# A kernel of attention and two expert layers: the experts' sums of tokens made at the end of the projection before, the first expert's results scaled afterwards

## The chip, the cores and the metric

The kernel runs on one core of one Trainium2 chip. The metric is the device time of one execution in microseconds (us), the median of several runs.

## The reference

Attention over 16 heads (2 batches of 8) with 576 positions of 64, then a gated layer, then eight experts that all see every token, mixed by a matrix P that is normalised by rows and columns eight times. All in float32.

```python
q_rot, k_rot = rotate(q), rotate(k)
scores = np.matmul(q_rot, k_rot.transpose(0, 1, 3, 2)) / np.sqrt(64)
attn = softmax(scores)                      # rows of 576
x = np.matmul(attn, v)                      # as 1152 tokens of 512

g = x @ w_gate                              # 512 -> 1536
x = (g / (1 + np.exp(-g)) * (x @ w_val)) @ w_out   # wo: 1536 -> 512

logits = x @ w_gate2                        # 512 -> 8
P = np.exp(logits - logits.max())
for _ in range(8):
    P /= P.sum(1, keepdims=True) + 1e-9
    P /= P.sum(0, keepdims=True) + 1e-9
    P *= N / E
for e in range(8):                          # 512 -> 1024 -> 512
    out += P[:, e:e+1] * (np.maximum(x @ w1[e], 0) @ w2[e])
```

## The kernel before

Four stages follow each other: the attention (eight pairs of heads, to about 165 us), gate and value (`gv`, to about 320 us), the projection with w_out, here called wo (to 395 us), and the experts.

Every large matmul is made of three, since operands are split into a high and a low part (`xh` and `xl`, `wh` and `wl`): high by high, high by low, low by high (`mm3`). ScalarE makes the high part by a cast, VectorE the low part by a subtraction (`sub`). Weights of gate, value and wo come as 64-bit numbers. `convert` turns a unit of 1024 of them into two parts: one load, two ScalarE and seven VectorE instructions.

wo goes over four blocks `d` of 128 outputs and three blocks `c` of 384 tokens, each 36 matmuls into one PSUM bank `po`. ScalarE casts a bank into `xh`, VectorE makes `xl` from it.

The experts are 16 passes `n`, two per expert, each over 512 of the 1024 hidden units. The first matmul of a pass is made in a form with seven products in place of eight for a 2 by 2 block (halves of the 512 inputs by halves of tokens): `product` numbers them 1 to 7, each 6 matmuls of 288 columns. Products 3, 5, 6 and 7 need sums and differences of quarters of x: `sums(c)` makes them for token block `c` (0 or 1, 576 tokens each) from `x32`, which is `xh + xl` again in one piece, and splits them into `sh` and `sl`. `plain` makes products 1 and 2, `rest` the other five, with VectorE's additions (`add`) between them. A relu leaves `hh` and `hl`. Then `w2_tile` makes one tile of y (128 tokens by 512, 12 matmuls) at a time; nine make a pass. VectorE multiplies it with the column of `Pm` of its expert and adds it to `acc`.

The gate, which makes `Pm`, runs inside the first pass as a generator: its TensorE instructions are put between others, one step at each count in `GSTEPS`. A step of the eight rounds is a `pc` matmul on TensorE, then eight small VectorE operations that end in the next `Pm`. While `Pm` is not ready, the y tiles of pass 0 stay in PSUM (list `y`).

The order on TensorE is that of the code. On the other engines a scheduler of the framework sets it when the kernel is built; each engine does its instructions strictly in that order. Pools of SBUF stand on each other like a stack; a pool that is opened where others lay waits until these are done with. The pools of the experts (`hp`, `sp`, `ep`, `wp2` and others) lie where `up` with the gated values `uh` and `ul` was.

Of the kernel before, what the change touches and what calls it, by code (L numbers as in the profile page):

```python
# [29 lines left out]
GSTEPS = {17, 20} | {24 + 4 * i for i in range(10)}  # L30
# [27 lines left out]
def fused(ctx, tc, qk, v, rope, wgv, wo, wg2, w1, w2, out):  # L58
# [55 lines left out]
    def convert(src, hi, lo, wide=False):  # L114
# [14 lines left out]
        last = nc.vector if wide else nc.gpsimd  # L129
# [390 lines left out]
    def gated(x, x2, ps, W, W1):  # L520
        nonlocal cvp
        with ExitStack() as st:
            cvp = pool("cvp", bufs=2, stack=st)
            up = pool("up", stack=st)
            tp = pool("tp", bufs=2, stack=st)
            uh = [up.tile([128, NT], F32R, name=f"uh{f}") for f in range(KF)]
            ul = [up.tile([128, NT], F32R, name=f"ul{f}") for f in range(KF)]

            def gv(f, c):
                if f not in W:  # L530
                    W[f] = load_w64(wgv[f])
                w = W[f]
                ts = slice(c * CH, c * CH + CH)
                pg = ps.tile([128, 512], F32, tag="a", name="pg")[:, 0:CH]
                pv = ps.tile([128, 512], F32, tag="a", name="pv")[:, 0:CH]
                for o, dst in ((0, pg), (512, pv)):
                    for kk in range(KD):
                        mm3(dst, w, (slice(None), slice(o + kk * 128, o + kk * 128 + 128)),
                            x, (slice(None), kk, ts), kk == 0, kk == KD - 1)
                sg = tp.tile([128, CH], F32, tag="sg", name="sg")  # L540
                nc.scalar.activation(out=sg, in_=pg, func=AF.Silu)
                nc.vector.tensor_tensor(out=sg, in0=pv, in1=sg, op=ALU.mult)
                nc.scalar.copy(out=uh[f][:, ts], in_=sg)
                sub(ul[f][:, ts], sg, uh[f][:, ts])

            order = [(f, c) for f in range(KF) for c in range(NC)]
            for f in range(2):
                if f not in W:
                    W[f] = load_w64(wgv[f])
            for n, (f, c) in enumerate(order):  # L550
                if c == 0 and f + 2 < KF and f + 2 not in W:
                    W[f + 2] = load_w64(wgv[f + 2])
                gv(f, c)
            O = {}
            nc.sync.dma_start(out=wr, in_=wg2)
            nc.scalar.copy(out=wg[:, :, 0], in_=wr)
            sub(wg[:, :, 1], wr, wg[:, :, 0])

            def o_unit(i):
                if i * 8 < KD * KF and i not in O:  # L560
                    O[i] = load_w64(wo[:, i * WU:(i + 1) * WU])

            o_unit(0)
            o_unit(1)
            xh, xl = x2
            for d in range(KD):
                for c in range(NC):
                    if d == KD - 1 and c == 0:
                        W1[0, 0] = winograd_w(load_raw(w1[0, :, 0:WU]))
                    ts = slice(c * CH, c * CH + CH)  # L570
                    po = ps.tile([128, 512], F32, tag="a", name="po")[:, 0:CH]
                    for kk in range(KF):
                        i, o = divmod(d * KF + kk, 8)
                        o_unit(i + 1)
                        mm3(po, O[i], (slice(None), slice(o * 128, o * 128 + 128)),
                            (uh[kk], ul[kk]), (slice(None), ts), kk == 0, kk == KF - 1)
                    nc.scalar.copy(out=xh[:, d, ts], in_=po)
                    sub(xl[:, d, ts], po, xh[:, d, ts])


    def experts(x, ps, W1):
# [3 lines left out]
        nonlocal cvp  # L585
        cvp = pool("raw", bufs=3)
        hp = pool("hp")
        sp = pool("sp")
        ep = pool("ep")
        wp2 = pool("wp2", bufs=2)  # L590
        p1p = pool("p1p", bufs=5)
        dp = pool("dp", bufs=3)
# [3 lines left out]
        x32 = ep.tile([128, KD, NT], F32, tag="acc", name="x32")  # L596
        Pm = ep.tile([128, NTT, E], F32, name="Pm")
# [14 lines left out]
        def halves(c):  # L612

            o = 2 * HC * c
            return slice(o, o + HC), slice(o + HC, o + 2 * HC), slice(HC * c, HC * c + HC)

        def sums(c):

            a, b, o = halves(c)
            r = slice(a.start, b.stop)  # L620
# [8 lines left out]
            def low(i):  # L629
                sub(sl[:, i, :, o], s[i], sh[:, i, :, o])  # L630
# [17 lines left out]
        def product(n, u, c, i, po):  # L648
# [6 lines left out]
            if n == 0:  # L655
                gate_step()
# [241 lines left out]
```

## Time and profile before

| | before |
|---|---|
| median of 3 runs | 1181.37 us (1178.01 to 1184.85) |
| the profiled execution | 1178.95 us |
| its span | 1177.2 us |
| TensorE (PE) busy | 1145.4 us, 97% |
| VectorE (DVE) busy | 818.2 us, 70% |
| ScalarE (ACT) busy | 378.7 us, 32% |
| GpSimd (POOL) busy | 90.0 us, all in the first 230 us |

The span is the profiled execution from its first to its last instruction; the time also has what lies around it. Busy shares are means over stages with different limits, so they are to be read by stage. PEclk is the share of TensorE's full clock that was granted. An engine's row can name what it waited for ("<-DVE Pm").

### The profile page before, as it was taken

To read this page: it belongs to the slowest core of one execution; us is meant where nothing else is said; L and a number is where in the kernel's file an instruction comes from. 1 tells how busy PE (TensorE), PEld (TensorE's weight loads), DVE (VectorE), ACT (ScalarE), POOL (GpSimd) and SP (SyncE) were. 2 spreads that over 40 slices of the span, in tenths; PEclk is the share of its full clock that TensorE was granted. 3 is DMA by queue.
4 is the path that set the end of the run, shared out by engine and by line. 5 is a ranking of instruction groups with operands and counts; after the bars stand their busy time and mean duration, and the time that the engine had idled before them with its cause. 6 is when DMAs were issued, how large, how long until landed. Compare 5 with 4: busy or idle time off the path is not lost.

```text
span 1177.2 us, 16921 instructions
## 1 busy us (share of the span) xinstructions
PE 1145.4 (97%) x6840; PEld 1033.7 (88%) x6840; DVE 818.2 (70%) x1380; ACT 378.7 (32%) x623; POOL 90.0 (8%) x88
## 2 busy tenths in 40 slices
PE   7999999999999888999999999999999999999998
PEld 6767779999999786988989989989899899898997
DVE  7787759998842696857757658567586585685763
ACT  4667654443311440312313223123122232131220
POOL 5567300000000000000000000000000000000000
PEclk7999999999999988999999999999999999999999
DMA  5876413333211100111111111111111111111002
GB/s 161 235 209 164 113 72 108 107 108 108 72 55 52 56 18 19 55 54 36 51 46 49 36 36 55 54 36 55 54 36 37 37 53 55 36 55 54 18 1 80
DMA packets 24125, 80.62 MB, mean 68 GB/s; under 512 B 4272, under 2 KB 4784, under 8 KB 21872
## 3 DMA queue, kind: packets, MB, share of 16 engines
q1 hardware_dynamic: 24048, 79.56, 22.4%
q8 instruction: 53, 0.87, 0.3%
q14 instruction: 24, 0.20, 0.0%
HBM read 64.80 MB, written 2.36 MB: 57 GB/s over the span
## 4 chain that ended last, share of the span: by engine, by line
PE 90%; DVE 5%; DMA 2%; issue 1%; SPq 1%; ACT 1%; POOL 0%; DVEq 0%
PE p L719 11%; PE p L720 11%; PE p L721 11%; PE s L268 4%; PE pv L380 3%; PE t L308 2%; PE po L159 2%; PE po L161 2%; PE po L160 2%; PE pg L161 2%; PE pg L159 2%; PE pv L161 2%; PE pg L160 2%; PE pv L159 2%; PE pv L160 2%
## 5 line engine op out<-in xcount | busy, mean ns | idle before, releaser
L719 PE MATMUL p<-wh,hh 128*128 128x512 f32 x576 | 226.4, 393 | 0.0
L720 PE MATMUL p<-wl,hh 128*128 128x512 f32 x576 | 225.6, 392 | 0.0
L721 PE MATMUL p<-wh,hl 128*128 128x512 f32 x576 | 225.5, 391 | 0.0
L100 ACT CAST wh<-raw 128x768 fp32r<-128x768 f32 (+1 forms) x96 | 94.0, 982 | 366.7 <-PE p L721 259.9
L728 DVE SCALAR_TENSOR_TENSOR acc<-p,Pm,acc 128x512 f32<-128x512 f32 x135 | 101.1, 749 | 156.6 <-PE p L721 156.6
L67 DVE TENSOR_TENSOR wl<-raw,wh 128x768 fp32r<-128x768 f32 (+1 forms) x96 | 108.6, 1131 | 41.6 <-ACT wh L100 40.6
L721 PEld LDWEIGHTS p<-wh,hl 128*128 128x128 f32 x576 | 109.0, 189 | 22.9
L719 PEld LDWEIGHTS p<-wh,hh 128*128 128x128 f32 x576 | 109.1, 189 | 22.2
L720 PEld LDWEIGHTS p<-wl,hh 128*128 128x128 f32 x576 | 109.1, 189 | 22.1
L663 ACT ACTIVATE hh<-d 128x1152 fp32r<-128x1152 f32 (+1 forms) x68 | 74.6, 1098 | 126.1 <-DVE d L668 126.0
L664 DVE SCALAR_TENSOR_TENSOR hl<-d,hh 128x1152 fp32r<-128x1152 f32 (+1 forms) x68 | 85.8, 1263 | 21.9 <-ACT hh L663 21.9
L273 DVE TENSOR_REDUCE ng<-s 128x1 f32<-128x576 f32 x72 | 54.0, 753 | 19.2 <-PE s L268 17.2
L289 ACT ACTIVATE p<-s,ng 128x576 f32<-128x576 f32 x64 | 47.6, 743 | 26.8 <-DVE ng L273 26.7
L111 DVE TENSOR_TENSOR raw<-raw 128x256 f32<-128x256 f32 x128 | 53.3, 417 | 0.7
L159 PE MATMUL pg<-xh,wh 128*128 128x384 f32 x144 | 48.8, 339 | 3.3 <-ACT wh L140 2.6
L160 PE MATMUL pg<-xl,wh 128*128 128x384 f32 x144 | 48.7, 338 | 0.0
L161 PE MATMUL pg<-xh,wl 128*128 128x384 f32 x144 | 48.6, 338 | 0.0
L160 PE MATMUL pv<-xl,wh 128*128 128x384 f32 x144 | 48.3, 335 | 0.0
L159 PE MATMUL pv<-xh,wh 128*128 128x384 f32 x144 | 48.3, 335 | 0.0
L161 PE MATMUL pv<-xh,wl 128*128 128x384 f32 x144 | 48.1, 334 | 0.0
L159 PE MATMUL po<-uh,wh 128*128 128x384 f32 x144 | 48.1, 334 | 0.0
L160 PE MATMUL po<-ul,wh 128*128 128x384 f32 x144 | 48.1, 334 | 0.0
(3328 smaller groups left out, 2692.8 us busy)
## 6 DMA issues: line engine op xcount, KB each, us to landing
raw<-in_w SPq DMA_DIRECT2D x64, 512.0 KB, 3.9
raw<-in_wgv SPq DMA_DIRECT2D x11, 1024.0 KB, 4.9
x<-in_qk SPq DMA_DIRECT2D x15, 576.0 KB, 4.7
raw<-in_wo SPq DMA_DIRECT2D x6, 1024.0 KB, 4.8
x<-hl SPq DMA_DIRECT2D x42, 144.0 KB, 3.7
x<-hl SPq DMA_DIRECT2D x14, 288.0 KB, 4.1
v<-in_v SPq DMA_DIRECT2D x8, 320.0 KB, 4.9
out<-acc SPq DMA_DIRECT2D x9, 256.0 KB, 2.0
```

The costliest lines, as they stand in the source:

```text
L67: (eng or nc.vector).tensor_tensor(out=out_, in0=a, in1=hi.bitcast(F32), op=ALU.subtract)
L100: nc.scalar.copy(out=hi[:, 0:n], in_=raw[:, 0:n])
L159: nc.tensor.matmul(ps, wh[wsl], xh[xsl], start=first, stop=False)
L160: nc.tensor.matmul(ps, wh[wsl], xl[xsl], start=False, stop=False)
L161: nc.tensor.matmul(ps, wl[wsl], xh[xsl], start=False, stop=last)
L273: nc.vector.tensor_reduce(out=R[n, u], in_=SC[n, u][:, :, 0:288], axis=AX.XY, op=ALU.max, negate=True)
L663: nc.scalar.activation(out=hh[:, f, ts], in_=src, func=AF.Relu)
L664: nc.vector.scalar_tensor_tensor(out=hl[:, f, ts], in0=src, scalar=0.0, in1=hh[:, f, ts].bitcast(F32), op0=ALU.max, op1=ALU.subtract)
L719: nc.tensor.matmul(po, hh[:, f, tl], wh[:, ws], start=f == 0, stop=False)
L720: nc.tensor.matmul(po, hh[:, f, tl], wl[:, ws], start=False, stop=False)
L721: nc.tensor.matmul(po, hl[:, f, tl], wh[:, ws], start=False, stop=f == 3)
L728: nc.vector.scalar_tensor_tensor(out=acc[:, t], in0=po, scalar=Pm[:, t, e:e + 1], in1=acc[:, t], op0=ALU.mult, op1=ALU.add)
```

## The change

- wo's tail: ScalarE also copies each bank `po` as float32 into `x32`. `sums` no longer adds `xh` and `xl`.
- `token_sums` makes the four sums in place in `x32`, one after the other; the casts and low parts follow.
- The first pass is done in another order: all products of the first 576 tokens and y tiles 0 to 3, then the second 576 and tiles 4 to 8. Each group stays together, and the logits stand between the `plain` parts of block 0 and 1.
- The y tiles of pass 0 are copied to `acc` by ScalarE as they are. Pass 1, the second half of the same expert, is added; afterwards the whole `acc` is scaled by `Pm` in place.
- `GSTEPS`: the steps of the gate are spread over passes 0 and 1.
- `up` and the experts' pools lie on the right side of SBUF, in an order in which what is needed first lies over the `uh`, `ul` that are free first, and wait tile by tile (`reuse_waits="tile"`).
- wo's weights are loaded and converted in units of 512, in the buffers of the experts' raw weights (`raw`, three of 4 KB), where a unit of 1024 had its own.

```diff
-GSTEPS = {17, 20} | {24 + 4 * i for i in range(10)}
+GSTEPS = {10, 14, 18} | {24 + 6 * i for i in range(9)}
...
-    def load_w64(src):
+    def load_w64(src, n=WU):
         hi, lo = new_w()
-        for _ in convert(src, hi, lo, wide=True):
-            pass
+        for cs in (slice(i, i + n) for i in range(0, WU, n)):
+            for _ in convert(src[:, cs], hi[:, cs], lo[:, cs], wide=n == WU):
+                pass
...
+            cvp = pool("raw", bufs=3, reuse_waits="tile")
+            ep = pool("ep", reuse_waits="tile")
+            x32 = ep.tile([128, KD, NT], F32, tag="acc", name="x32")
+            w_out(x2, x32, ps, uh, ul, W1)
...
+    def token_sums(x32, c):
+        a, b, _ = token_halves(c)
+        a11, a12, a21, a22 = (x32[:, k:k + 2, ts] for ts in (a, b) for k in (2, 0))
+        for o, p, q, op in ((a22, a21, a22, ALU.add), (a21, a11, a21, ALU.subtract),
+                            (a11, a22, a11, ALU.subtract), (a12, a12, a11, ALU.subtract)):
+            nc.vector.tensor_tensor(out=o, in0=p, in1=q, op=op)
+        return a22, a11, a21, a12
...
-                O[i] = load_w64(wo[:, i * WU:(i + 1) * WU])
+                O[i] = load_w64(wo[:, i * WU:(i + 1) * WU], 512)
...
                 nc.scalar.copy(out=xh[:, d, ts], in_=po)
                 sub(xl[:, d, ts], po, xh[:, d, ts])
+                nc.scalar.copy(out=x32[:, d, ts], in_=po)
...
+        sp, hp, wp2, p1p, dp, sm = (pool(name, bufs=bufs, side="right", reuse_waits="tile") for name, bufs in
+                                    (("sp", 1), ("hp", 1), ("wp2", 2), ("p1p", 5), ("dp", 3), ("small", 1)))
...
         def sums(c):
-            nc.vector.tensor_tensor(out=x32[:, :, r], in0=xh[:, :, r].bitcast(F32), in1=xl[:, :, r].bitcast(F32), op=ALU.add)
+            s = token_sums(x32, c)
+            o = token_halves(c)[2]
+            for i in (1, 2, 0, 3):
+                nc.scalar.copy(out=sh[:, i, :, o], in_=s[i])
                 sub(sl[:, i, :, o], s[i], sh[:, i, :, o])
...
             if n == 0:
-                y.append((po, t))
+                nc.scalar.copy(out=acc[:, t], in_=po)
+            elif n == 1:
+                add(acc[:, t], po, acc[:, t])
             else:
...
                 if n == 0:
                     sums(0)
+                    plain(0, 0, 0)
+                    next(g)
+                    next(g)
+                    plain(0, 0, 1)
+                    next(g)
+                    sums(1)
                     load1(0, 1)
...
                     for c in range(2):
                         for u in range(2):
+                            if u:
+                                plain(0, u, c)
                             rest(0, u, c, dp.tile([128, 4, HC], F32, tag="d", name="d"))
...
+                        for t in (range(4), range(4, NTT))[c]:
+                            w2_tile(0, t)
...
+                if n == 1:
+                    for _ in g:
+                        pass
+                    for t in range(NTT):
+                        nc.vector.tensor_scalar(out=acc[:, t], in0=acc[:, t], scalar1=Pm[:, t, 0:1], scalar2=None,
+                                                op0=ALU.mult)
```

What the scheduler makes of it is seen at three places. A row has the line, the operation, the tiles written and read, the size, and the engines whose signal it waits for. First, VectorE at the end of wo, before. L621 is the sum of `xh` and `xl` into x32, L626 a sum of quarters, L668 an addition behind a product.

```order
L67 TENSOR_TENSOR wl<-raw,wh 128x768 [waits DMAHW3_49,PE_49,Activation_49]
L111 TENSOR_TENSOR raw<-raw 128x256 [waits DVE_49] x4
L621 TENSOR_TENSOR x_4228<-xh,xl 128x4x576 [waits PE_49]
L67 TENSOR_TENSOR wl<-raw,wh 128x1024 [waits Activation_49]
L67 TENSOR_TENSOR xl<-po,xh 128x384 [waits Activation_49]
L67 TENSOR_TENSOR wl<-raw,wh 128x1024 [waits DMAHW4_49,Activation_49]
L626 TENSOR_TENSOR x_4228<-x_4228 128x2x288 [waits DVE_49]
L67 TENSOR_TENSOR wl<-raw,wh 128x1024 [waits DMAHW5_49,Activation_49]
L668 TENSOR_TENSOR c_4270<-p__4271,p_4268 128x288 [waits PE_49,Activation_49]
L621 TENSOR_TENSOR x_4228<-xh,xl 128x4x576 [waits DVE_49]
L668 TENSOR_TENSOR c_4290<-p__4291,p_4288 128x288 [waits PE_49,Activation_49]
```

The same place in the changed kernel; L582 is a sum of quarters in `token_sums`.

```order
L67 TENSOR_TENSOR xl<-po,xh 128x384 [waits Activation_49] x3
L582 TENSOR_TENSOR x_3641<-x_3641 128x2x288 [waits Activation_49]
L582 TENSOR_TENSOR x_3641<-x_3641 128x2x288 [waits DVE_49]
L67 TENSOR_TENSOR wl<-raw,wh 128x768 [waits DMAHW1_49,PE_49,Activation_49]
L582 TENSOR_TENSOR x_3641<-x_3641 128x2x288 [waits DVE_49]
L111 TENSOR_TENSOR raw<-raw 128x256 [waits DVE_49]
L582 TENSOR_TENSOR x_3641<-x_3641 128x2x288 [waits DVE_49]
L111 TENSOR_TENSOR raw<-raw 128x256 [waits DVE_49] x2
L67 TENSOR_TENSOR xl<-po,xh 128x384 [waits Activation_49]
L111 TENSOR_TENSOR raw<-raw 128x256 [waits DVE_49]
L67 TENSOR_TENSOR sl<-x_3641,sh 128x2x288 [waits Activation_49] x4
L67 TENSOR_TENSOR wl<-raw,wh 128x1024 [waits DMAHW2_49,PE_49,Activation_49]
```

The first row of before with `xl` (after L621) is wo's last one; in the changed kernel it is the row with a single `xl`. The whole sum of 4 x 576 columns is gone, and the four sums of quarters of block 0 stand ahead of the last `xl`, between the parts of a weight.

Second, VectorE inside a round of the gate in the first pass, before: L769 to L771 are three of the round's small operations, `Pm` the matrix, L664 the low part of a relu, L111 a difference of weights.

```order
L668 TENSOR_TENSOR d<-p__4596,d 128x288 [waits DVE_49]
L769 TENSOR_SCALAR rs<-rs 128x9 [waits DVE_49]
L668 TENSOR_TENSOR d<-p__4605,d 128x288 [waits DVE_49,PE_49]
L111 TENSOR_TENSOR raw<-raw 128x256 [waits DVE_49]
L668 TENSOR_TENSOR d<-p__4613,d 128x288 [waits DVE_49,PE_49]
L770 RECIPROCAL rs<-rs 128x9 [waits DVE_49]
L111 TENSOR_TENSOR raw<-raw 128x256 [waits DVE_49]
L664 SCALAR_TENSOR_TENSOR hl<-d,hh 128x576 [waits Activation_49]
L771 TENSOR_TENSOR Pm<-Pm,rs 128x72 [waits DVE_49]
L664 SCALAR_TENSOR_TENSOR hl<-d,hh 128x288 [waits Activation_49]
L67 TENSOR_TENSOR wl<-raw,wh 128x1024 [waits Activation_49]
```

In the changed kernel the fourth round (L778 to L780, L784) stands in the second token block of the pass, between the additions (L674) behind products 6, 7 and 5.

```order
L674 TENSOR_TENSOR p_4737<-p__4751,p_4737 128x288 [waits DVE_49,PE_49]
L670 SCALAR_TENSOR_TENSOR hl<-c_4739,hh 128x288 [waits Activation_49]
L111 TENSOR_TENSOR raw<-raw 128x256 [waits DVE_49]
L778 TENSOR_SCALAR rs<-rs 128x9 [waits DVE_49]
L674 TENSOR_TENSOR d<-p__4759,p_4737 128x288 [waits DVE_49,PE_49]
L674 TENSOR_TENSOR d<-p__4767,p_4737 128x288 [waits PE_49]
L111 TENSOR_TENSOR raw<-raw 128x256 [waits DVE_49]
L779 RECIPROCAL rs<-rs 128x9 [waits DVE_49]
L674 TENSOR_TENSOR d<-p__4767,d 128x288 [waits DVE_49]
L780 TENSOR_TENSOR Pm<-Pm,rs 128x72 [waits DVE_49]
L784 TENSOR_REDUCE cs<-pc 128x8 [waits PE_49]
```

Before, a round's `Pm` followed the last addition of the pass and part of its relus; now rounds stand among the additions of products that TensorE has still to make.

Third, TensorE at the `pc` of a round: before, the first of them, between the last product of the pass (`p__4613`) and the first y tile (`p_4649`).

```order
L160 MATMUL p__4613<-xl,wh 128x288
L161 MATMUL p__4613<-xh,wl 128x288
L774 MATMUL pc<-Pm,ones 128x72 [waits DVE_49]
L719 MATMUL p_4649<-wh,hh 128x512 [waits DMAHW4_49,DMAHW5_49,DMAHW3_49,DMAHW6_49,DMAHW2_49,DMAHW7_49,DMAHW1_49,DMAHW0_49]
L720 MATMUL p_4649<-wl,hh 128x512
L721 MATMUL p_4649<-wh,hl 128x512
```

In the changed kernel the fourth `pc` stands between products 5 and 3 of the last group.

```order
L163 MATMUL p__4767<-sh,wh 128x288
L164 MATMUL p__4767<-sl,wh 128x288
L165 MATMUL p__4767<-sh,wl 128x288
L783 MATMUL pc<-Pm,ones 128x72 [waits DVE_49]
L163 MATMUL p__4786<-sh,wh 128x288 [waits PE_49]
L164 MATMUL p__4786<-sl,wh 128x288
L165 MATMUL p__4786<-sh,wl 128x288
```

The `pc` moved from the y tiles into the products, and waits for VectorE at both places. The first y tile no longer waits for all DMA queues.

## Rows read from the trace of the kernel before

**Rows 1.** The page, part 1: engine, busy us, share of the span, instructions.

```profile
PE 1145.4 (97%) x6840; PEld 1033.7 (88%) x6840; DVE 818.2 (70%) x1380; ACT 378.7 (32%) x623; POOL 90.0 (8%) x88
```

**Rows 2.** TensorE's waits: line, releaser: us in total, times, longest.

```profile
PE pc L774 <- DVE Pm L771: 7.1, 4, 2.6
...
PE p__4399 L160 <- DVE sl L67: 2.6, 1, 2.6
PE p__4281 L160 <- DVE xl L67: 2.1, 1, 2.1
```

**Rows 3.** By stretch: us; PE, PEld, DVE, ACT, POOL busy; clock; DMA share, GB/s.

```profile
318.50:395.29 76.79, 76.79 (x445) 76.79 (x445) 29.22 (x40) 13.69 (x21) 0.00 (x0) 1.00 0.13 42
395.29:472.05 76.76, 63.22 (x329) 53.62 (x329) 61.53 (x151) 23.73 (x38) 0.00 (x0) 0.89 0.11 35
472.05:518.79 46.74, 46.74 (x277) 42.51 (x276) 31.90 (x56) 11.75 (x14) 0.00 (x0) 1.00 0.16 46
```

**Rows 4.** The same view: three stretches of low clock.

```profile
413.30:420.10 6.80, 6.80 (x33) 6.80 (x33) 6.54 (x13) 2.02 (x4) 0.00 (x0) 0.57 0.00 0
437.20:440.60 3.40, 3.40 (x11) 2.56 (x10) 3.37 (x13) 0.15 (x1) 0.00 (x0) 0.64 0.50 142
457.70:464.50 6.80, 6.02 (x17) 4.92 (x18) 5.20 (x13) 0.00 (x0) 0.00 (x0) 0.57 0.00 0
```

**Rows 5.** TensorE's timeline: start us, us, engine, line, operation [idle before <-releaser].

```profile
395.29 0.29 PE L159 MATMUL p__4261<-xh,wh 128*128 128x288 f32 x1
...
396.07 0.30 PE L159 MATMUL p__4271<-xh,wh 128*128 128x288 f32 x1
...
399.70 0.40 PE L160 MATMUL p__4281<-xl,wh 128*128 128x288 f32 x1 [2.15 <-DVE xl L67]
...
400.87 0.33 PE L741 MATMUL plt<-xh,wg 128*16 128x384 f32 x1
...
405.04 0.29 PE L159 MATMUL p__4332<-xh,wh 128*128 128x288 f32 x1
...
412.95 0.61 PE L160 MATMUL p__4399<-sl,wh 128*128 128x288 f32 x1 [2.61 <-DVE sl L67]
...
435.96 0.47 PE L774 MATMUL pc<-Pm,ones 128*128 128x72 f32 x2 [2.63 <-DVE Pm L771]
```

**Rows 6.** VectorE's groups in the first pass: count | busy us, mean ns | idle before.

```profile
L67 DVE TENSOR_TENSOR wl<-raw,wh 128x1024 fp32r<-128x1024 f32 x6 | 7.3, 1220 | 1.7 <-ACT wh L100 1.7
...
L827 DVE TENSOR_SCALAR acc<-p,Pm 128x512 f32<-128x512 f32 x8 | 5.6, 747 | 4.5 <-PE p L721 4.5
L621 DVE TENSOR_TENSOR x<-xh,xl 128x2304 f32<-128x2304 f32 x2 | 5.1, 2554 | 0.7 <-PE po L161 0.7
...
L768 DVE TENSOR_REDUCE rs<-Pm 128x9 f32<-128x72 f32 x8 | 1.8, 227 | 0.2
```

**Rows 7.** VectorE's timeline, three instructions in a row.

```profile
405.33 0.45 DVE L668 TENSOR_TENSOR c<-p__4291,p 128x288 f32<-128x288 f32 x1
405.70 0.74 DVE L626 TENSOR_TENSOR x<-x 128x576 f32<-128x576 f32 x1
406.37 0.75 DVE L67 TENSOR_TENSOR sl<-x,sh 128x576 fp32r<-128x576 f32 x1
```

**Rows 8.** ScalarE's groups in the first pass.

```profile
L627 ACT CAST sh<-x 128x576 fp32r<-128x576 f32 x8 | 5.4, 673 | 4.0 <-DVE x L626 3.9
```

**Rows 9.** VectorE's groups in the attention: conversions of 512 columns.

```profile
L134 DVE TENSOR_SCALAR cv<-cv 128x512 uint32<-128x512 uint32 x2 | 3.1, 1529 | 0.1
...
L137 DVE SCALAR_TENSOR_TENSOR cv<-raw,cv 128x512 uint32<-128x512 uint32 x2 | 1.4, 685 | 0.0
...
L141 DVE TENSOR_SCALAR raw<-cv 128x512 uint32<-128x512 uint32 x2 | 0.8, 414 | 0.0
```

**Rows 10.** The page, part 6: DMA issues, KB each, median us to landing.

```profile
raw<-in_w SPq DMA_DIRECT2D x64, 512.0 KB, 3.9
...
raw<-in_wo SPq DMA_DIRECT2D x6, 1024.0 KB, 4.8
```

More of the change, by code (lines that the diff above doesn't have):

```diff
@@ L121, in convert @@
             a = cvp.tile([128, WU], F32, tag="cv", name="cv")
+        elif cvp is not None:
+            raw = cvp.tile([128, WU], F32, tag="cv", name="raw64").bitcast(U32)
+            a = cvp.tile([128, WU], F32, tag="cv", name="cv")[:, 0:512]
         else:
@@ L128, in convert @@
         au = a.bitcast(U32)
-        last = nc.vector if wide else nc.gpsimd
+        last = nc.gpsimd if cvp is None else nc.vector
         yield
@@ L581, in experts @@
[L581 to L592, printed above, removed]
+        with ExitStack() as right:
+            up = pool("up", stack=right, side="right")
+            uh, ul = zip(*[(up.tile([128, NT], F32R, name=f"uh{f}"), up.tile([128, NT], F32R, name=f"ul{f}"))
+                           for f in reversed(range(KF))][::-1])
+            with ExitStack() as st:
+                gate_val(x, ps, W, uh, ul, st)
+            cvp = pool("raw", bufs=3, reuse_waits="tile")
+            ep = pool("ep", reuse_waits="tile")
+            x32 = ep.tile([128, KD, NT], F32, tag="acc", name="x32")
+            w_out(x2, x32, ps, uh, ul, W1)
@@ new lines, in gated, with gate_val, gv @@
+        return ep, x32
+    def gate_val(x, ps, W, uh, ul, st):
+        nonlocal cvp
+        cvp = pool("cvp", bufs=2, stack=st)
+        tp = pool("tp", bufs=2, stack=st)
+        def gv(f, c):
+            if f not in W:
+                W[f] = load_w64(wgv[f])
+            w = W[f]
+            ts = slice(c * CH, c * CH + CH)
+            pg = ps.tile([128, 512], F32, tag="a", name="pg")[:, 0:CH]
+            pv = ps.tile([128, 512], F32, tag="a", name="pv")[:, 0:CH]
+            for o, dst in ((0, pg), (512, pv)):
+                for kk in range(KD):
+                    mm3(dst, w, (slice(None), slice(o + kk * 128, o + kk * 128 + 128)),
+                        x, (slice(None), kk, ts), kk == 0, kk == KD - 1)
+            sg = tp.tile([128, CH], F32, tag="sg", name="sg")
+            nc.scalar.activation(out=sg, in_=pg, func=AF.Silu)
+            nc.vector.tensor_tensor(out=sg, in0=pv, in1=sg, op=ALU.mult)
+            nc.scalar.copy(out=uh[f][:, ts], in_=sg)
+            sub(ul[f][:, ts], sg, uh[f][:, ts])
+        order = [(f, c) for f in range(KF) for c in range(NC)]
+        for f in range(2):
+            if f not in W:
+                W[f] = load_w64(wgv[f])
+        for n, (f, c) in enumerate(order):
+            if c == 0 and f + 2 < KF and f + 2 not in W:
+                W[f + 2] = load_w64(wgv[f + 2])
+            gv(f, c)
@@ new lines, in w_out, with o_unit @@
+    def w_out(x2, x32, ps, uh, ul, W1):
+        O = {}
+        nc.sync.dma_start(out=wr, in_=wg2)
+        nc.scalar.copy(out=wg[:, :, 0], in_=wr)
+        sub(wg[:, :, 1], wr, wg[:, :, 0])
+        def o_unit(i):
+            if i * 8 < KD * KF and i not in O:
+                O[i] = load_w64(wo[:, i * WU:(i + 1) * WU], 512)
+        o_unit(0)
+        o_unit(1)
+        xh, xl = x2
+        for d in range(KD):
+            for c in range(NC):
+                if d == KD - 1 and c == 0:
+                    W1[0, 0] = winograd_w(load_raw(w1[0, :, 0:WU]))
+                ts = slice(c * CH, c * CH + CH)
+                po = ps.tile([128, 512], F32, tag="a", name="po")[:, 0:CH]
+                for kk in range(KF):
+                    i, o = divmod(d * KF + kk, 8)
+                    o_unit(i + 1)
+                    mm3(po, O[i], (slice(None), slice(o * 128, o * 128 + 128)),
+                        (uh[kk], ul[kk]), (slice(None), ts), kk == 0, kk == KF - 1)
+                nc.scalar.copy(out=xh[:, d, ts], in_=po)
+                sub(xl[:, d, ts], po, xh[:, d, ts])
+                nc.scalar.copy(out=x32[:, d, ts], in_=po)
@@ L839, in fused @@
     W1 = {}
-    gated(xT, x2, ps, W, W1)
-    experts(x2, ps, W1)
+    ep, x32 = gated(xT, x2, ps, W, W1)
+    experts(x2, x32, ep, ps, W1)
 def _tables():
```

120 lines of the change are left out of this document (21 added, 99 removed).

## The prediction

> **What bounds the kernel now.** I read the busy times first: TensorE works 97% of the span [rows 1], so only its idle time and its slow clock can be won. The list of TensorE's waits says for whom it waits [rows 2]: besides waits at the start, the large ones are on VectorE's tiles, `Pm` of the gate (7.1 us in 4 waits), `sl` (2.6) and `xl` (2.1), all after wo's end. A table by stretch then compares two passes of the experts [rows 3]: the first (n = 0, with the gate inside) takes 76.76 us, TensorE busy 63.22 of them at a mean granted clock of 0.89; the next takes 46.74 us, wholly busy, at 1.00. The slow stretches of the clock came last [rows 4]: in three, of 6.8, 3.4 and 6.8 us, the mean is about 0.6, that is mostly the lower level of 1.2 GHz. The timeline shows what stood ahead of them [rows 5]: a wait of 2.15 us ended at 399.70 and no drop followed; 2.61 us, shortly after another wait on `sh`, ended at 412.95 and the clock was low from 413.3; 2.63 us ended at 435.96 and it was low from 437.2.
>
> What would the first pass take without waits? A product starts every 0.78 us, and the 24 logit matmuls take 4.17 from 400.87 to 405.04 [rows 5]. It is a pass of 46.74 [rows 3] plus 4.17 plus about 2.1 for the gate's transposes and small matmuls (`pt`, `pm`, `pb`, eight pairs `pc`; an estimate): 53.0. Hence 23.8 us are lost there: 13.5 idle (76.76 - 63.22), some 8 to the half clock (16.2 busy us in 17.0 [rows 4]), the rest at seams. VectorE is busy 61.5 us in this pass [rows 3], more than TensorE needs in all: the pass is VectorE's.
>
> **The change part by part.** All prices are those of one profiled execution: 1178.95 us, span 1177.2; the median of the three runs is 2.4 us above it.
>
> *x32 and the sums.* Two adds of `xh` and `xl`, 2554 ns each [rows 6], go: 5.1 us on VectorE just where `xl` and `sl` are waited for. In their place ScalarE copies each wo tile once more, twelve times under 0.67 us (its price for 576 columns [rows 8]; these have 384). It was busy 13.69 of that stage's 76.79 us [rows 3], so this costs nothing. The four sums of the first 576 tokens (0.67 each back to back, 405.70 to 406.37 [rows 7]) now stand ahead of the last `xl`: 2.7 us leave the pass.
>
> *Scaling.* Nine scalings of 747 ns [rows 6], 6.0 us back to back, leave the first pass. ScalarE copies y instead, nine times at about that price, while a y tile takes TensorE (46.74 - 28 x 0.78)/9 = 2.8 us. Pass 1 gets nine scalings out of SBUF, between 0.41 each (a 512-wide operation there [rows 9]) and 0.75 (the PSUM form [rows 6]): 3.7 to 6.7 us on a VectorE busy 31.9 of 46.7 there [rows 3]; nothing. So VectorE owes 61.5 - 5.1 - 2.7 - 6.0 = 47.7 us in a pass that TensorE could do in 53.0. That fits, but 90% full, so its queue has to be followed.
>
> *The ledger*, from T = wo's end (395.29 [rows 5]), in the changed order, each instruction at its row's price, back to back (0.37 for an add, 0.67 for 576 columns [rows 7], 1.13 for a weight of 1220 ns [rows 6]). T to T+7.3: four products and the 24 logit matmuls. The last `xl` stands four rows from the sums now and needs only `xh`, cast by T+0.7; it is done by T+1.3 and wanted at T+4.4: **no wait** where 2.15 stood. The four `sh` casts (0.67 [rows 8]) are done by T+3.1, `sl` by T+4.4, two w2 weights by T+6.6. TensorE enters the second group at T+7.3 with `sh` and `sl` ready: **no wait** where `sl` held it. Then VectorE falls behind, with four second sums, three `sl`, one more weight, relus and adds:
> - TensorE does ten products and nine transposes (0.66) and stands at the transpose `pm` from T+15.9; `mx` is done at T+16.9: 1.1 us.
> - The first y tile needs the relu of products just done: 1.3 us.
> - With two more products and y tiles 0 to 3 TensorE is at T+31.4; the gate's rounds (eight small operations of 0.23 [rows 6], some 2.1 us with their gaps) fit beside them.
> - In the second half TensorE does ten products and one `pc` and is at the fourth `pc` at T+39.4. VectorE starts with the first of them at T+32.4 and has 11 adds (4.1), three relus (1.4), a weight of 768 columns (0.9), its four differences (1.4) and seven small operations ahead of the fourth round's `Pm`, with what it waits for products ready at T+42.5: 3.1 us.
> - Behind tile 4 the fifth `pc` finds `Pm` behind two relus and four differences: 0.3 + 2.3 us.
>
> The last tile ends at T+61.1: 53.0 and 8.1 of waits. After the 3.1 us I expect one drop of 3.4 us, as after 2.63 [rows 4, 5]. It costs up to 1.7, and part of that comes off the next wait, since VectorE catches up: 1.0. The pass is 62.1 in place of 76.8: **14.7 us won**.
>
> A rule of the Trainium skill speaks against the waits that are left. The page "TensorE: Matmul & The Clock Gate", part 1, says that the throttled clock is the default and that sustained activity is what lifts it, so a wait can cost more than itself; this trace agrees for the waits of 2.61 and 2.63 us and not for the 2.15. If every one of the four waits brought a drop, it would be 1.7 us three times more, 5 us; by the rows the two short ones bring none.
>
> *Pools by their own bytes.* Before, the pools of `x32`, `sh`, `hh` and w2's tiles lay over `up`, and the first add of `x32` waits for wo's last matmul. Now each tile waits for the `up` tiles below it. In the order ScalarE still does the last `xh` ahead of the `sh` casts, so I give this nothing beyond the ledger; what it costs if such a wait stays is the second rival.
>
> *wo in halves.* Six loads of 1 MB become twelve of 512 KB (median landing 4.8 and 3.9 us [rows 10]) into three 4 KB buffers, and each conversion holds two of them. On VectorE a half costs 3 x 0.41 + 4 x 0.69 = 4.0 us [rows 9]; at the slowest row, 1.53 for two of them, 6.2 [rows 9]. That row is from the attention, the one stage where GpSimd works, so I take the low end. With 0.7 of ScalarE ahead of it, and a quarter of VectorE's time for the gate's own tiles (two of 384 columns, some 0.55 each, per unit), a half takes 6.3 to 9.2 us. In the new order twelve of 36 gate units (24 matmuls of 0.174, 4.2 us) stand behind the last gate weight, then 75 us of wo until T, and the twelfth half is wanted at T-16.6: 50 + 75 - 16.6 = 108 us for twelve, 9.0 each. Free at 6.3, 2 us late at 9.2: I take nothing and keep 2 for the range.
>
> The page "DMA: Bandwidth & Descriptors", "Anatomy of one DMA", gives each transfer about 2 us fixed, so six more transfers would be 12 us on the path. By the rows a pair costs 2 x 3.9 - 4.8 = 3.0 us more, 18 in all, and both hide in the 2.7 us of slack per half.
>
> **Sum.** 1178.95 - 14.7 = 1164.3 on the profiled execution's scale; with half or all of the 2.4 us by which the median lies above it, 1165.5 to 1166.7. I say 1166. Bounds of the same mechanism: without the two late waits (5.7) and the drop, 55.4 us of pass, so 1158 to 1160; with two drops of 6.8 us, 67.9, so 1170 to 1172.5.
>
> **The rivals.**
> - *The waits only move* (0.13). VectorE is 90% booked, and the eight `pc` now lie among its adds. For it: before, every wait at a `pc` was VectorE's queue (7.1 us in four). If three more rounds are as late as the one of 2.63, with its drop, 3 x (2.6 + 1.7) = 12.9 us go back: 1177 to 1179, no change.
> - *The sums do not come loose* (0.10), the change doing not what it says. If the last `xl` or `sl` still waits, by a pool's wait or ScalarE's order, the waits of 2.15, 2.61 and that on `sh` (4.2 with it) and their drop (3.4) stay, 9.7 back less the 1.1 of `pm`: 1173 to 1175. Against it: the last `xl` has nothing but four short rows between it and the sums.
> - *wo's halves come late* (0.06), the other side. Place: TensorE in wo's last two blocks, on `wh` and `wl`. Each microsecond over 9.0 per half costs 12. From 10.7 on the gain and 6 us more are gone; at 11 it is 1164 + 24 = 1188. For it: the upper end of 9.2; against: GpSimd rests there, and DMA is busy 0.13 of the stage [rows 3].
> - *VectorE's order is kinder than the ledger* (0.11): a pass of 55 to 57 us, 1157 to 1160.
>
> **How the numbers follow.** The forecast has 0.60, with a range of its own from 1160 to 1172. The three runs of before lie 7 us apart; a measurement of this kernel can tell about 0.5% (5.9 us) from no change. Faster (under 1175.5): 0.60 + 0.11 + 0.08 of the second rival = 0.79; same: 0.13 + 0.02 = 0.15; slower: 0.06. The range leaves out half of the last rival below 1158, and above 1177 the third and most of the first, 0.05 + 0.06 + 0.09 = 0.20.
>
> **What would show it.** The first pass (first expert product to the first of pass 1) takes 60 to 64 us; no wait on `xl` or `sl` is over 0.5 us; the waits are on `mx`, the relu of y tile 0 and two `Pm`; the clock is low once or twice, not three times; pass 1 stays at 46.7; none on wo's weights. I am wrong if the pass stays above 70 us, if TensorE idles inside wo, or if pass 1 grows.

## The result and the profile after

The changed kernel took 1165.95 us (median of 4 runs, 1163.12 to 1172.19), the kernel before 1183.09 us beside it (4 runs, 1178.01 to 1184.85): a ratio of 0.9876, 95% interval 0.9837 to 0.9914. Two later batches gave 0.9878 (0.9845 to 0.991) and 0.99 (0.9866 to 0.9934). The forecast was 1166, range 1158 to 1177.

The page's first part of the profiled execution (1172.19 us) answers to [rows 1]: TensorE's work is unchanged, VectorE's nearly so, and ScalarE has 14 us more.

```profile
span 1170.4 us, 17008 instructions
...
PE 1146.6 (98%) x6840; PEld 1033.4 (88%) x6840; DVE 816.7 (70%) x1420; ACT 392.3 (34%) x656; POOL 89.9 (8%) x88
```

This span is only 6.8 us shorter than before's, because this execution lost 8.7 us ahead of the changed stages: the first expert product starts at 404.04, where it started at 395.29 [rows 5]. The last section shows that this is no effect of the change. So the experiments are read by the time from the first expert product to the end of the span, which holds none of it: 781.88 us before (1177.17 - 395.29), **766.37 after** (1170.41 - 404.04), 15.5 us won. Both are single executions. The table by stretch of the kernel after, with the columns of [rows 3], says where: the first pass, the second, the third, and wo.

```profile
404.04:464.69 60.65, 55.62 (x327) 47.18 (x327) 47.26 (x136) 28.16 (x47) 0.00 (x0) 1.00 0.14 44
464.69:511.69 47.00, 47.00 (x280) 42.76 (x279) 35.07 (x67) 12.23 (x15) 0.00 (x0) 1.00 0.16 45
511.69:558.40 46.71, 46.71 (x277) 42.52 (x276) 32.11 (x56) 11.84 (x14) 0.00 (x0) 1.00 0.15 46
329.20:404.04 74.84, 74.84 (x434) 74.84 (x433) 36.66 (x65) 20.53 (x37) 0.00 (x0) 1.00 0.20 58
```

The first pass went from 76.76 to 60.65 us, at the full clock throughout (0.89 before); the second grew by 0.3, to 47.0, with the round of the gate that moved there; the third is as before, and so is wo (74.9 us from its first matmul to its end in both kernels; the stretch of [rows 3] begins 1.9 us ahead of it). TensorE's waits in the first pass, which answer to [rows 2]: those on `xl` and `sl` are gone, and `Pm` has 4.1 us in place of 7.1.

```profile
PE pc L783 <- DVE Pm L780: 4.1, 2, 2.4
...
PE pm L764 <- DVE mx L761: 0.4, 1, 0.4
PE p L725 <- ACT hh L669: 0.4, 1, 0.4
```

VectorE's timeline at the end of wo and just behind it shows how `xl` came loose. The sums of quarters (L582) stand ahead of the last `xl`, which ends 1.3 us behind wo's end; the four `sl` of block 0 end at 408.3, and TensorE wants them at 411.4.

```profile
401.95 0.75 DVE L582 TENSOR_TENSOR x<-x 128x576 f32<-128x576 f32 x1
402.62 0.42 DVE L111 TENSOR_TENSOR raw<-raw 128x256 f32<-128x256 f32 x1
402.95 0.75 DVE L582 TENSOR_TENSOR x<-x 128x576 f32<-128x576 f32 x1
403.62 0.88 DVE L111 TENSOR_TENSOR raw<-raw 128x256 f32<-128x256 f32 x2
404.75 0.56 DVE L67 TENSOR_TENSOR xl<-po,xh 128x384 fp32r<-128x384 f32 x1 [0.25 <-ACT xh L609]
405.22 0.41 DVE L111 TENSOR_TENSOR raw<-raw 128x256 f32<-128x256 f32 x1
405.55 2.76 DVE L67 TENSOR_TENSOR sl<-x,sh 128x576 fp32r<-128x576 f32 x4
408.23 2.35 DVE L67 TENSOR_TENSOR wl<-raw,wh 128x1024 fp32r<-128x1024 f32 x2
```

### The profile page after: what moved, and what is told of

It is laid out like the page before. It is cut to its first block, busy times and chain, and to the rows that moved or that the text cites. A ratio compares the mean times of both kernels' runs of the same rounds, so it can differ in the third digit from the quotient of the medians.

```text
span 1170.4 us, 17008 instructions
## 1 busy us (share of the span) xinstructions
PE 1146.6 (98%) x6840; PEld 1033.4 (88%) x6840; DVE 816.7 (70%) x1420; ACT 392.3 (34%) x656; POOL 89.9 (8%) x88
## 4 chain that ended last, share of the span: by engine, by line
PE 91%; DVE 4%; DMA 2%; issue 1%; ACT 1%; SPq 1%; POOL 0%; DVEq 0%; ACTq 0%
PE p L727 11%; PE p L725 11%; PE p L726 11%; PE s L272 4%; PE pv L384 3%; PE t L312 2%; PE po L163 2%; PE po L164 2%; PE po L165 2%; PE pg L165 2%; PE pg L163 2%; PE pv L165 2%; PE pg L164 2%; PE pv L164 2%; PE pv L163 2%
## 5 line engine op out<-in xcount | busy, mean ns | idle before, releaser
L737 DVE SCALAR_TENSOR_TENSOR acc<-p,Pm,acc 128x512 f32<-128x512 f32 x126 | 94.4, 749 | 146.6 <-PE p L727 146.6
L111 DVE TENSOR_TENSOR raw<-raw 128x256 f32<-128x256 f32 x128 | 53.4, 417 | 0.6
L165 PE MATMUL po<-uh,wl 128*128 128x384 f32 x144 | 48.4, 336 | 0.0
```

What stands on the lines that cost most here:

```text
L165: nc.tensor.matmul(ps, wl[wsl], xh[xsl], start=False, stop=last)
L737: nc.vector.scalar_tensor_tensor(out=acc[:, t], in0=po, scalar=Pm[:, t, e:e + 1], in1=acc[:, t], op0=ALU.mult, op1=ALU.add)
```

## The experiments

In each, "the first pass" and "to the end" are the two stretches above (60.65 and 766.37 us in the kernel after). Edits are against the kernel after, where nothing else is said.

**1. Pools that don't wait tile by tile.**

```diff
-            cvp = pool("raw", bufs=3, reuse_waits="tile")
-            ep = pool("ep", reuse_waits="tile")
+            cvp = pool("raw", bufs=3)
+            ep = pool("ep")
...
-        sp, hp, wp2, p1p, dp, sm = (pool(name, bufs=bufs, side="right", reuse_waits="tile") for name, bufs in
+        sp, hp, wp2, p1p, dp, sm = (pool(name, bufs=bufs, side="right") for name, bufs in
```

> The changed kernel with its pools waiting as whole pools again (the new places kept). Measure: the first expert pass, first product to first product of pass 1, 60.65 us in the changed kernel. Theory V (the gain is work taken off VectorE's queue; ScalarE does the last xh ahead of the sh casts anyway): 60 to 62 us, no wait on sh or sl over 0.5 us. Theory P (what frees the start of the pass is that each tile waits for its own bytes alone): the waits on sh and sl of before return, 4.2 us and a stretch of low clock, 66 us or more.

First pass 60.64, to the end 766.36 us, the waits the same to 0.01. That the pools wait tile by tile is worth nothing beside the others. The places of the pools stay the new ones here, so what these are worth is not tested (experiment 3 has more on it).

**2. y copied by VectorE.** The same copies, on the engine that the change relieved of the scaling.

```diff
-                nc.scalar.copy(out=acc[:, t], in_=po)
+                nc.vector.tensor_copy(out=acc[:, t], in_=po)
```

> The changed kernel, but the nine y tiles of pass 0 are copied to acc by VectorE (6.0 us in all) and not by ScalarE. Theory V, taken as an amount alone: 6 us more of VectorE, a pass of 64 to 66 us. Theory V read by place: y tiles stand where VectorE waits for TensorE, so the copies fall into its gaps: 60.5 to 62 us.

First pass 60.74, to the end 766.45. VectorE is busy 4.9 us more than after, and TensorE loses 0.1:

```profile
395.00:455.74 60.74, 55.70 (x328) 47.09 (x328) 52.15 (x144) 23.45 (x39) 0.00 (x0) 1.00 0.14 44
```

**3. x32 added by VectorE again.** Everything else stays, the order too.

```diff
-                nc.scalar.copy(out=x32[:, d, ts], in_=po)
...
+            a, b, o = token_halves(c)
+            r = slice(a.start, b.stop)
+            nc.vector.tensor_tensor(out=x32[:, :, r], in0=xh[:, :, r].bitcast(F32), in1=xl[:, :, r].bitcast(F32), op=ALU.add)
             s = token_sums(x32, c)
-            o = token_halves(c)[2]
```

> The changed kernel, but VectorE adds xh and xl into x32 again (two adds of 2.55 us in sums) and ScalarE's twelve copies are gone. Theory V: VectorE's backlog in the first token block grows by 5 us and shows at pm and at the first y tile: a pass of 64 to 66 us, perhaps with a stretch of low clock. Theory O (it is the order of products and tiles that hides VectorE, its amount is not felt): 62 us or less.

First pass 65.72, to the end 771.44: 5.07 us lost. VectorE has 4.6 us more to do in the pass, about as much as in the experiment before; here it comes ahead of `sl`, and the wait on `sl` is back, with two stretches of low clock (mean 0.95 in the pass).

```profile
395.89:461.61 65.72, 58.67 (x328) 50.07 (x328) 51.83 (x140) 27.76 (x46) 0.00 (x0) 0.95 0.14 41
```

```profile
PE pc L784 <- DVE Pm L781: 3.2, 2, 2.4
...
PE p__4422 L164 <- DVE sl L67: 2.5, 1, 2.5
```

One of the two stretches of low clock stands behind the wait on `sl`, the other behind the wait of 2.38 us on `Pm`. The second comes in some executions of the kernel after, too, and costs 0.64 us there (experiment 10), so the edit itself costs 4.4 to 5.1.

VectorE's timeline shows that the two adds (L640) did not cost the same. Wo ends at 395.89 here.

```profile
390.36 0.56 DVE L67 TENSOR_TENSOR xl<-po,xh 128x384 fp32r<-128x384 f32 x1 [5.68 <-ACT xh L609]
390.95 2.56 DVE L640 TENSOR_TENSOR x<-xh,xl 128x2304 f32<-128x2304 f32 x1
...
396.98 0.55 DVE L67 TENSOR_TENSOR xl<-po,xh 128x384 fp32r<-128x384 f32 x1
...
399.11 2.55 DVE L640 TENSOR_TENSOR x<-xh,xl 128x2304 f32<-128x2304 f32 x1
...
405.23 1.42 DVE L67 TENSOR_TENSOR sl<-x,sh 128x576 fp32r<-128x576 f32 x2
```

The first add ran 5 us ahead of wo's end, where VectorE had been idle. In the kernel before it could not: it waited for wo's last matmul, and with a weight it stood ahead of the last `xl`.

```profile
395.49 2.56 DVE L621 TENSOR_TENSOR x<-xh,xl 128x2304 f32<-128x2304 f32 x1 [0.66 <-PE po L161]
397.96 1.22 DVE L67 TENSOR_TENSOR wl<-raw,wh 128x1024 fp32r<-128x1024 f32 x1
399.10 0.55 DVE L67 TENSOR_TENSOR xl<-po,xh 128x384 fp32r<-128x384 f32 x1
```

So the wait on `xl` stays away in this experiment though VectorE adds as before: ScalarE's copies are not needed to remove it. What lets the add start early is most likely the new place of `x32`, which before lay over `up`; no run has that alone. What costs the time is the second add and the sums of quarters that slid behind wo's end, all ahead of the `sl` that TensorE waited for until 406.03.

So 4.9 us of work on VectorE cost 0.1 in one place and 4.6 us cost 4.4 to 5.1 in another: its load in the pass is not what sets the time, but what stands ahead of the instruction that TensorE wants next.

**4. The late scaling alone**, in the kernel before: y copied by ScalarE, pass 1 added, `acc` scaled afterwards, the rounds of the gate six counts apart over both passes.

```diff
-GSTEPS = {17, 20} | {24 + 4 * i for i in range(10)}
+GSTEPS = {17, 20} | {24 + 6 * i for i in range(10)}
...
-                y.append((po, t))
+                nc.scalar.copy(out=acc[:, t], in_=po)
+            elif n == 1:
+                add(acc[:, t], po, acc[:, t])
...
+                if n == 1:
+                    for _ in g:
+                        pass
+                    for t in range(NTT):
+                        nc.vector.tensor_scalar(out=acc[:, t], in0=acc[:, t], scalar1=Pm[:, t, 0:1], scalar2=None, op0=ALU.mult)
```

> The kernel before with one part of the change alone: y tiles of pass 0 copied to acc by ScalarE, pass 1 added, the scaling by Pm afterwards, and the gate's steps spread over passes 0 and 1 (every sixth count). Pools, x32, wo and the order of pass 0 as before. If the parts add up: the waits on xl, sh and sl with their low clock stay (about 9.7 us), those on Pm go (7.1 us and 5 us of low clock): a pass of 64 to 68 us where before had 76.8. If only all parts together help, since the first tiles then meet VectorE's backlog: 72 us or more.

To the end 770.95 us, 10.9 better than before: first pass 64.71, second 47.87. The waits on `sl` and `xl` stand as in [rows 2]; those on `Pm` fell from 7.1 us to 2.2.

```profile
PE p__4399 L160 <- DVE sl L67: 2.6, 1, 2.6
...
PE pc L776 <- DVE Pm L773: 2.2, 3, 1.2
PE p__4281 L160 <- DVE xl L67: 2.1, 1, 2.1
PE p__4399 L159 <- ACT sh L627: 1.6, 1, 1.6
```

Part of the 10.9 can be chance: the waits on `sh` and `sl` are those of before, but the low clock behind them lasted 6.8 us there [rows 4] and 3.4 here (mean 0.53 in the 3.4 us from 413.00, 1.00 from 421 on). At half the clock that is worth up to 1.7 us, by estimate. So the late scaling gives 9.2 to 10.9 us and `x32` in experiment 3 4.4 to 5.1, together 13.6 to 16.0, where the whole gives 15.5. The two are not the exact complements of each other (experiment 3 keeps the places of the pools, this one the old order), so the sum shows no more than that nothing large is missing.

**5. The old steps of the gate** in the kernel after: all rounds in the first pass, four counts apart.

```diff
-GSTEPS = {10, 14, 18} | {24 + 6 * i for i in range(9)}
+GSTEPS = {17, 20} | {24 + 4 * i for i in range(10)}
```

> The changed kernel with the gate's steps of before (counts 17, 20, then every fourth). Theory V with its queue: more rounds meet VectorE's additions, 3 to 6 us more of waits at pc, 64 to 67 us, perhaps one stretch of low clock. If where the rounds stand is of no account: 60 to 61.

First pass 65.01, to the end 770.51: 4.1 us lost. Three waits on `Pm` (5.6 us in all, the longest 3.0, with low clock behind it) and 1.5 on the relu. The late scaling pays because the rounds need no longer be done by the first pass's y tiles.

**6. All 28 products first, then the nine y tiles**, as before; the order of the products stays the new one.

```diff
-                        for t in (range(4), range(4, NTT))[c]:
-                            w2_tile(0, t)
...
+                    for t in range(NTT):
+                        w2_tile(0, t)
```

> The changed kernel with all nine y tiles of pass 0 behind all 28 products (tiles 0 to 3 no longer between the halves); steps of the gate at the same counts. Theory O (the order hides VectorE's backlog behind four y tiles): TensorE waits among the last products and at the first tile for 5 to 8 us more, 66 to 69 us, with low clock. Theory V by amount alone: unchanged within 1.5 us, 59 to 62.

First pass 59.90, to the end 765.62: 0.75 better than the kernel after, though 3.4 us of it were at the low clock. The theory by which the order matters, with its 66 to 69 us of first pass, falls: with these steps the y tiles between the halves bring nothing. The order of the products was not tested alone.

```profile
403.44:463.34 59.90, 56.47 (x327) 48.95 (x327) 47.60 (x136) 28.21 (x47) 0.00 (x0) 0.97 0.14 45
```

**7. Rounds moved out of the late part of the pass**, as a try to win the two waits on `Pm` that are left.

```diff
-GSTEPS = {10, 14, 18} | {24 + 6 * i for i in range(9)}
+GSTEPS = {10, 14, 18, 24, 30, 36, 54, 60, 96, 102, 108, 114}
```

> The changed kernel with the rounds moved away from the second token block and tile 4: pc at counts 24, 30, 36, 54, 60 and, in pass 1's tiles, 96, 102, 108. If the two waits left at pc (2.38 and 1.73 us) come only from where the rounds stand: a first pass of 56 to 57.5 us, pass 1 as it was (47.0), 3 to 4 us faster than the changed kernel. If VectorE's amount of work sets the end of the pass, the waits move to the relu of tile 4 and the pass stays at 60.

First pass 57.37, but second 49.78, to the end 765.88: of 3.3 us won in the first pass 2.8 are lost in the second, where a `pc` waits 1.95 us.

```profile
404.04:461.41 57.37, 55.06 (x324) 46.61 (x323) 45.02 (x120) 27.84 (x47) 0.00 (x0) 1.00 0.15 47
461.41:511.19 49.78, 47.83 (x284) 43.13 (x282) 37.93 (x83) 12.21 (x15) 0.00 (x0) 1.00 0.14 43
```

VectorE's timeline ahead of that wait, which ended at 492.87: the `cs` of a round begins at 487.56 and the next `Pm` at 492.58, and between them lie the low part of a relu (1.35 us), an addition to `acc` and a conversion of 1.23 us. The end of it:

```profile
489.83 0.64 DVE L674 TENSOR_TENSOR acc<-p,acc 128x512 f32<-128x512 f32 x1
490.38 0.22 DVE L788 SCALAR_TENSOR_TENSOR Pm<-Pm,cs 128x72 f32<-128x72 f32 x1
490.64 0.23 DVE L777 TENSOR_REDUCE rs<-Pm 128x9 f32<-128x72 f32 x1
490.99 1.23 DVE L67 TENSOR_TENSOR wl<-raw,wh 128x1024 fp32r<-128x1024 f32 x1
...
492.58 0.23 DVE L780 TENSOR_TENSOR Pm<-Pm,rs 128x72 f32<-128x72 f32 x1
```

Its median of 6 runs, 1168.71 us, is 0.9899 of before (0.9863 to 0.9935), no better than the kernel after beside it (experiment 10).

**8. Rounds inside the y tiles**: three `pc` in tiles 0 to 3, one among the products behind them, three in tiles 4 to 8, the last at the start of pass 1. ("Quantiser rounds" in the text below means these rounds of the gate.)

```diff
-GSTEPS = {10, 14, 18} | {24 + 6 * i for i in range(9)}
+GSTEPS = {10, 14, 18, 23, 27, 31, 36, 53, 57, 61, 66, 72}
```

> The kernel after, its quantiser rounds in the first expert's pass and behind it put at the counts 10, 14, 18, 23, 27, 31, 36, 53, 57, 61, 66, 72: a round of weights never stands ahead of a statistic, a y tile's conversion or the scaling that TensorE is about to want. Theory P (the waits left over come from where the rounds stand, not from VectorE's amount of work): the two waits on a y tile's statistic (2.4 and 1.7 us in the kernel after) shrink below 1 us together, the first pass takes at most 58 us, the second pass stays at 46.7 to 47.2, since the last rounds are done well before the count 96 at which the run with moved rounds waited; from the first expert product to the end some 763 us against 766.4. Theory A (VectorE has too much to do in that stretch, and a moved round moves the wait): the first pass or the second keeps the 3 to 4 us, and the time from the first product to the end stays at 765.5 to 767.

First pass 57.88, second 46.99, to the end 763.61: 2.8 us better than the kernel after, with no wait on `Pm` at all. The same kernel again, with the kernel after beside it:

> The kernel after with the rounds at the counts 10, 14, 18, 23, 27, 31, 36, 53, 57, 61, 66, 72, timed beside the kernel after on the same chip. Theory P (waits come from where the rounds stand): 763.0 to 764.0 us from the first expert product to the end, first pass 57.5 to 58.5 us, about 2.8 us less than the kernel after, median some 1161 us where the start's low clock falls alike. Theory A (the one look was chance): 765.5 us or more.

> The kernel after unchanged, for comparison on the same chip: 766.0 to 767.1 us from the first expert product to the end, first pass 60.6 to 61.3 us, median some 1164 us where the start's low clock falls alike.

It took 1161.36 us (6 runs; ratio to before 0.9844, 0.9809 to 0.9879); the kernel after took 1168.45 there, 4 us over what was expected of its median. The profile of experiment 8's kernel repeats its first one to 0.03 us: 763.58 to the end, against 767.19. So the gain of this version over the kernel after is 2.8 to 3.6 us, of the 7.1 between the medians; the rest is probably the start (last section), but only one execution of each has a trace here. The two stretches and the waits that are left:

```profile
399.94:457.82 57.88, 55.62 (x328) 47.14 (x328) 47.98 (x135) 27.84 (x47) 0.00 (x0) 1.00 0.14 46
457.82:504.81 46.99, 46.99 (x280) 42.76 (x278) 35.17 (x68) 12.22 (x15) 0.00 (x0) 1.00 0.15 46
```

```profile
PE p L725 <- ACT hh L669: 0.9, 2, 0.5
PE p L727 <- DVE hl L670: 0.8, 1, 0.8
```

VectorE is as busy in this pass as in the kernel after (47.98 and 47.26) and TensorE exactly so (55.62). So the waits on `Pm` were a matter of where the rounds stand.

**9. The same with the tiles last.** The edit of experiment 6 and rounds at 10, 14, 18, 33, 37, 41, 45, 49, 53, 57, 61, 66.

> All 28 products of the first halves first and then the nine y tiles, as in the run with the tiles last, with the rounds at the counts 10, 14, 18, 33, 37, 41, 45, 49, 53, 57, 61, 66. Theory P (waits come from where the rounds stand): the wait of 2.4 us in that run goes, no low clock, first pass 57 to 58 us, second pass 46.7 to 47.2, and 763 us from the first product to the end: the order of tiles and halves makes no difference to it. Theory A (VectorE's amount of work): the wait moves to another tile or into the second pass, and the time from the first product to the end stays at 765 to 767.

First pass 59.78, to the end 765.27, with a wait of 2.77 us on `Pm` and 3.4 us of low clock. The time is the one that theory A gave. The wait did not go: ahead of its `Pm` VectorE had two weights (1.17 and 0.95) and two low parts of relus (0.76 and 0.45) to do. Only one set of steps was tried in this order, so whether it could be as good as experiment 8 is open.

**10. The kernel after again.**

> The changed kernel once more, beside the one with moved steps on the same chip: first pass 60 to 61 us; 0.985 to 0.99 of the time before. If the 34 us of low clock at the start of its first profile come from the change, they are there again; if they are chance, this profile has a stretch nearer to the 14 us of before.

1163.55 us (6 runs, 1163.05 to 1171.76), ratio 0.9878. First pass 61.29, to the end 767.01; the difference of 0.64 us to the first profile is the clock's:

```profile
438.40:441.80 3.40, 3.40 (x14) 3.40 (x15) 2.52 (x6) 1.81 (x3) 0.00 (x0) 0.50 0.10 10
```

```profile
438.39 0.70 PE L783 MATMUL pc<-Pm,ones 128*128 128x72 f32 x2 [2.38 <-DVE Pm L780]
445.72 0.44 PE L783 MATMUL pc<-Pm,ones 128*128 128x72 f32 x2 [0.96 <-DVE Pm L780]
```

The same wait of 2.38 us was now followed by 3.4 us at 1.2 GHz (0.50 granted), and the next one shrank from 1.73 to 0.96.

## Why the prediction was right

In the main the mechanism was the one forecast, and the ledger can be held against the trace point by point (T is wo's end, 404.04 in the kernel after). Two of its reasons were not the right ones: why the late scaling pays and, in part, what frees `xl`.

| step | forecast | measured |
|---|---|---|
| last `xl` done, wait | T+1.3, none | T+1.3, none |
| `sl` of block 0 done, wait | T+4.4, none | T+4.3, none |
| two w2 weights done | T+6.6 | T+6.5 |
| `mx` done, wait at `pm` | T+16.9, 1.1 us | T+16.7, 0.44 us |
| relu for the first y tile | 1.3 us | 0.42 us |
| fourth `pc`: start, wait | T+42.5, 3.1 us | T+42.2, 2.38 us |
| fifth `pc`: wait | 0.3 + 2.3 us | 1.73 us |
| low clock | one of 3.4 us, costs 1.0 | none; 0.64 and 0.83 in two other executions |
| VectorE busy in the pass | 47.7 us | 47.26 us |
| first pass | 62.1 us | 60.65, 61.29, 61.48 us in three executions |
| first product to the end | 781.88 - 14.7 = 767.2 us | 766.37, 767.01, 767.19 us |

That the median came within 0.1 us of 1166 is luck. The medians of the kernel after in three batches were 1165.95, 1163.55 and 1168.45 us, those of before 1183.09, 1178.77 and 1181.19, so the gain was 17.1, 15.2 and 12.7 us; the forecast had 14.7 to 15.4 (from 1181.37). What can be held against the forecast more closely is the time behind the start, 0.0 to 0.8 us below it.

- *Two terms were mis-sized and cancel.* The gate's small matmuls were put at 2.1 us. TensorE's busy time in the pass, less a plain pass and the logits, is 55.62 - 46.71 - 4.17 = 4.7; the groups of the kernel after in that stretch have 2.6 for seven pairs of `pc` alone:

```profile
L783 PE MATMUL pc<-Pm,ones 128*128 128x72 f32 x14 | 2.6, 265 | 4.1 <-DVE Pm L780 4.1
```

  The waits came to 5.0 us where the ledger had 8.1. That is in good part one error, not two: at `pm` and at the fourth `pc`, where the ledger gives both sides, VectorE was 0.2 and 0.3 us earlier than there and TensorE 0.4 later, so it waited 0.7 less at each. Where VectorE sets the moment, a mis-sized TensorE term moves a wait and not the end.
- *x32 and the sums*: 5.1 us on VectorE and the waits on `xl` and `sl`. Experiment 3 gives 4.4 to 5.1 for x32 alone, the wait on `sl` (2.5 us) and the low clock behind it among them; that much is shown. The wait on `xl` is another matter: the prediction has it go with the adds, and in experiment 3, with the adds back on VectorE, it did not return. There the first add started 5 us ahead of wo's end. The prediction saw that before it waited for wo's last matmul, but gave the pools nothing of their own; their new places most likely allow the early start, which is not tested alone.
- *Scaling*: the step "6.0 us leave VectorE" named the wrong reason. Experiment 2 puts 4.9 us back and loses 0.1. What pays is that nothing in the first pass needs the last `Pm` any more, so that the rounds can be spread (experiment 4, 9.2 to 10.9 us in the kernel before; experiment 5, 4.1 for the steps alone in the kernel after). The nine scalings behind pass 1 took 0.48 us each, inside the forecast's 0.41 to 0.75. Pass 1 grew by 0.3 us, a sign that the prediction had set against itself: one round moved there (its `pc` starts at 466.27), which the forecast had not counted.
- *The order of halves and tiles* had no term of its own. Experiment 6 shows that the gain doesn't need the y tiles between the halves; with them experiment 8 found better places for the rounds than experiment 9, one set of steps, without them.
- *Pools*: nothing forecast, and nothing found for the waits tile by tile (experiment 1); their new places are not tested alone.
- *wo in halves*: nothing forecast, 2 us kept for the range. The halves were in time: the last conversion ended at 371.0, and the twelfth half was wanted at T-16.6 = 387.4, so 16 us were left; back to back a half took 6.2 us (seven from 293.6 to 336.8), the forecast's low end. A half landed in 3.8 us (the page of the kernel after) beside 4.8 for the whole [rows 10], so by estimate 2 x 3.8 - 4.8 = 2.8 us of a landing did not shrink with the size, and all of it was hidden: TensorE never waits on wo's weights. The page "DMA: Bandwidth & Descriptors", "Anatomy of one DMA", in the Trainium skill, gives a transfer a fixed cost of about 2 us, but its section is on transfers that GpSimd issues; these are issued by SyncE (SPq in [rows 10]), and the measured landings decide.
- *The rivals.* That the sums don't come loose and that the halves come late are excluded by the trace. "The waits only move": in the change itself those on `Pm` fell from 7.1 to 4.1 us; in experiment 7 they did move, into the second pass, at a smaller price than the rival's (2.8 us). "VectorE's order kinder" (55 to 57 us of pass) is nearly experiment 8 (57.88), which came there by other steps.

## What to carry to other kernels

A vector engine that is 80% busy in a stage has room, and lacks it only at the places where TensorE wants a result: 4.9 us of copies cost 0.1, and an add of 2.6 us in the idle time ahead of wo's end delayed nothing, while a second add and the sums behind it, ahead of the next product's operand, cost 4.4 to 5.1. So walk both queues row by row from the stage's start, and look for the dependent small chain (here the rounds of the gate) that can be put where the queue is empty; a table of numbers for it was worth 4 us here, and better numbers another 3. When such a chain moves, check the next stage for the same wait before calling it a gain.

## What the runs showed of the chip

- *The start's low clock differs between executions of one kernel*, and with it everything behind. In the first profile of the kernel after, the granted clock stayed at 0.50 (1.2 GHz) for 34.1 us; in the next one of the same kernel, for 13.7, as in the kernel before:

```profile
11.70:45.80 34.10, 30.77 (x126) 23.63 (x126) 20.59 (x30) 14.89 (x36) 14.72 (x13) 0.50 0.55 149
```

```profile
11.80:25.50 13.70, 10.63 (x46) 8.97 (x47) 11.86 (x16) 5.89 (x14) 5.54 (x5) 0.50 0.31 93
```

  The first expert product started at 404.04 and 396.20. Experiment 8's kernel had 13.7 us in one execution and 27.3 in the other, and its first product at 394.78 and 399.94. The times of one kernel spread accordingly (1163.12 to 1172.19). What decides it was not found; a comparison of single executions of this kernel can be wrong by 8 to 9 us, over half of what the change gives (the third execution of the kernel after had its first product at 394.95).
- *Whether a wait brings the clock down differs too.* The same wait of 2.38 us on the same instruction was followed or overlapped by low clock in three executions (experiments 3 and 10, and the one beside experiment 8), and in three it was not (the first profile and experiments 1 and 2); the waits on `Pm` of 2.41 (experiment 6), 2.77 (9) and 3.0 us (5) all were. In two of the three executions the drop can be priced against the kernel after without it: 0.64 us (3.4 us of low clock) and 0.83 us (6.8 us), no more, because the later wait on VectorE shrank; in the second of these it was gone. The page "TensorE: Matmul & The Clock Gate", part 1, in the Trainium skill, says that the throttled clock is the default and that activity lifts it. By that rule, which the prediction weighed, a wait can cost more than itself; here it did in some executions and not in others.
